# Two batches' query groups in one 512-column product for seven of twelve portions of a gate-and-value layer

## The chip, the cores and the metric

The kernel runs on one core of a Trainium2 chip. The metric is the time of one execution on the device, in microseconds (us); shorter is better.

## What is computed

Causal attention with a decaying bias, and then two gated expert layers on all tokens; the first normalises its input.

```python
x = attention(q, k, v, s)               # 4 batches, 8 heads, 576 tokens, 64 wide
x = x.transpose(0, 2, 1, 3).reshape(4 * 576, 512)
xn = x / sqrt(mean(x * x) + 1e-6) * rms_g
x = (silu(xn @ w_gate) * (xn @ w_val)) @ w_out      # 512 -> 1536 -> 512
return (silu(x @ w2_gate) * (x @ w2_val)) @ w2_out  # 512 -> 1536 -> 512
```

All is float32. A product is made of three: each factor is split into a high part H and a rest L, and HH + HL + LH is summed.

## The kernel before

**Groups.** The 576 queries of a batch are two groups, A (256 queries) and B (320). The change concerns group A of batches 0 and 1, called 0A and 1A here; 0B is group B of batch 0, and so on. Attention comes in the order 0A, 1A (`attend_early`), 0B, 1B, and then batches 2 and 3 with both groups at once. After a group's attention `normalise` turns its columns into `xH` and `xL` (512 features in four blocks k of 128 rows), in one of two slots: slot 0 holds 0A and then 0B, slot 1 holds 1A and then 1B, and so on.

**The first expert layer.** `moe1` makes the hidden features in twelve portions f of 128. A portion of a group is called a row here ("0A5" is portion 5 of 0A). `gate_value` makes its gate and its value: each 4 blocks k times 3 matmuls (HH, HL, LH), so 24 matmuls (L1071), into two of four rotating PSUM banks `mo`. `hidden` then takes one ScalarE operation (L1078) and two of VectorE (L1080, L1083), and the result goes to memory.

**What sets the order.** A planner (`Plan.run`) lists all operations by their dependences, a cost for each, and a priority, and writes one fixed order for each engine. Attention stands before rows: rows of 0A and 1A have the priority `P_MOE + f`, behind all attention, so they fill TensorE (PE) where attention leaves it free. `hidden` has the highest priority. A row can only be placed once its group is normalised and its weights are loaded.

**Steps that the prediction names**, all in `normalise`: L1038 and L1039 (VectorE) write the factors of the rows, L1043 transposes them (PE), L1046 (ScalarE) copies them into the last block of the slot's own `xL`, L1051 spreads them over the features (PE), L1055 (VectorE) multiplies, L1058 (ScalarE) writes `xH`, L1060 (POOL or VectorE) writes `xL`. As L1046 writes into the slot, it must wait until the last row of the group that held the slot before has read it. In attention, L651 and L776 are scores, L720 and L795 transposes, L732 values. L1440 is a product of the layer's second half, with 512 columns.

Of the kernel before, what the change touches and what calls it, by code (L numbers as in the profile page):

```python
# [11 lines left out]
F32R = mybir.dt.float32r  # L12
# [5 lines left out]
ACTF = mybir.ActivationFunctionType  # L18
ALU = mybir.AluOpType
# [4 lines left out]
P = 128  # L24
DM, DFF = 512, 1536
KD, KF = DM // P, DFF // P
# [8 lines left out]
GROUPS = {"A": (0, 256, (0, 1)), "B": (256, 320, (2, 3, 4))}  # L35
# [5 lines left out]
PE, DVE, ACT, POOL, SP, NONE = "PE", "DVE", "ACT", "POOL", "SP", "NONE"  # L41
# [38 lines left out]
class Plan:  # L80
# [20 lines left out]
    def op(self, eng, ns, fn, r=(), w=(), pri=0.0, later=0, port=False, slow=0.0):  # L101

        n = len(self.ops)
        done = 0
        if eng == SP:  # L110
            took = ns / self.RATE
            ns = max(450.0, took)
            done = 2300.0 + took - ns + slow
        deps, shared = set(), []
        for accesses, writes in ((r, False), (w, True)):
            for a in accesses:
                buf, part = a if isinstance(a, tuple) else (a, None)
                key = buf if isinstance(buf, str) else buf.key
                live = self.live.setdefault(key, [])
                keep = []  # L120
                for part2, m, wrote in live:
                    meets = part is None or part2 is None or part == part2
                    if meets and (writes or wrote) and m != n:
                        deps.add(m)
                    if not (writes and meets and (part is None or part == part2)):
                        keep.append((part2, m, wrote))
                keep.append((part, n, writes))
                self.live[key] = keep
                if not isinstance(buf, str) and buf.share is not None and buf not in shared:
                    shared.append(buf)  # L130
                    buf.uses += 1
        engs = eng if isinstance(eng, list) else [(eng, ns)]
        self.ops.append((engs, fn, deps, pri, done, shared, later, port))
        return n
# [132 lines left out]
def c_mm(n):  # L267
    return max(72.0, 0.4167 * n + 13.3)
# [6 lines left out]
def c_tt(n):  # L275
    return 75 + 1.04 * n
# [6 lines left out]
def c_act(n, aps=0):  # L283
    return 60 + 0.83 * n + 93 * aps
# [16 lines left out]
def tile_kernel(  # L301
# [16 lines left out]
    op = plan.op  # L318
# [32 lines left out]
    def bank(tag):  # L351
        return buf("ps", tag, [P, 512], F32)
# [49 lines left out]
    P_CONV, P_MOE, P_ATT = -1.0e3, 1.0e4, 0.0  # L402
# [55 lines left out]
    def raw_places(last):  # L458

        return {(f, z): buf("w", f"{'HL'[z]}{f + 2}", [P, 1024], I32, f"raw{z}")  # L460
                if f + 2 < KF else last[z] for f in range(KF) for z in range(2)}

    def load_gv(src, f, places, tmps, pri, early=None, after=()):
        H, L = (buf("w", f"{z}{f}", [P, 1024], F32R) for z in "HL")
        for z in range(2):
            convert(src[f, :, 512 * z:512 * z + 512], (H, L), z, places[f, z], tmps(), pri,
                    early, after)
        return H, L
# [451 lines left out]

    xHL = [[buf("m1", f"x{z}{i}", [P, KD, 320], F32R) for z in "HL"] for i in range(2)]

    def normalise(i, g, tot, pri, split=True):
        pri -= 2
# [134 lines left out]
                out=L()[:, k, :n], in0=x()[:, k, :n], in1=f32(H()[:, k, :n]), op=ALU.subtract),  # L1061
               r=halves + [(H, k)], w=[(L, k)], pri=pri, port=True)

    def gate_value(ps, W, X, f, z, n, pri, also=(), after=()):

        wH, wL = W
        xH, xL = X
        for k in range(KD):
            c = slice((z * KD + k) * P, (z * KD + k + 1) * P)
            for i, (a, x) in enumerate(((wH, xH), (wH, xL), (wL, xH))):  # L1070
                op(PE, c_mm(n), lambda en, a=a, x=x, c=c, k=k, i=i: en.matmul(  # L1071
                    ps()[:, :n], a()[:, c], x()[:, k, :n], start=(k == 0 and i == 0),
                    stop=(k == KD - 1 and i == 2)), r=[(a, z), (x, k), *after],
                   w=[ps] if k or i else [ps, *also], pri=pri)

    def hidden(gp, vp_, t, hh, n, pri):

        op(ACT, c_act(n), lambda en: en.activation(t()[:, :n], gp()[:, :n], ACTF.Tanh, scale=0.5),  # L1078
           r=[gp], w=[t], pri=pri)
        op(DVE, c_tt(n), lambda en: en.scalar_tensor_tensor(  # L1080
            out=t()[:, :n], in0=t()[:, :n], scalar=1.0, in1=gp()[:, :n], op0=ALU.add,
            op1=ALU.mult), r=[gp, t], w=[t], pri=pri)
        op(DVE, c_tt(n), lambda en: en.tensor_tensor(  # L1083
            out=hh()[:, :n], in0=t()[:, :n], in1=vp_()[:, :n], op=ALU.mult),
           r=[vp_, t], w=[hh], pri=pri)

    h_parts = {}

    def moe1(groups, W, pri, post, deep=None, hook=None):

        for f in range(KF):
            for b, g, i in groups:
                q0, n, _ = GROUPS[g]
                tok = b * S + q0
                k = next(deep) if deep else 0
                if k % 2:
                    gp, vq = (bank(f"{('sps', 'tp')[k // 2 % 2]}{z}") for z in range(2))
                    t, hh = deep_t[k // 2 % 2]
                else:
                    gp, vq = mo_bank(), mo_bank()  # L1100
                    t = shared("m1", "t", 2, [P, 320], F32)
                    hh = shared("m1", "hh", 2, [P, 320], F32)
                gate_value(gp, W[f], xHL[i], f, 0, n, pri + f, [vq, f"row {b}{g}{f}"])
                gate_value(vq, W[f], xHL[i], f, 1, n, pri + f)
                hidden(gp, vq, t, hh, n, post)
                for t0, m, gi, at in SPANS:
                    lo, hi = max(t0, tok), min(t0 + m, tok + n)
                    if lo < hi:
                        h_parts.setdefault(gi, set()).add(lo)
                        op(SP, 4 * P * (hi - lo),  # L1110
                           lambda en, gi=gi, lo=lo, hi=hi, t0=t0 - at, tok=tok, f=f, hh=hh: en.dma_start(
                               out=h_d[gi][f, :, lo - t0:hi - t0], in_=hh()[:, lo - tok:hi - tok]),
                           r=[hh], w=[(f"h_d{gi}", (f, lo))], pri=post, later=1200)
            if hook is not None:
                hook(f)

# [1 line left out]
    W1 = []  # L1120
    plan.live["ex"] = []
    places = raw_places([buf("ex", f"ex{i}", [P, 1024], I32, f"cvs{i}") for i in range(2)])
# [10 lines left out]
    def attend_early(b, x, tot):  # L1133
        for h in range(NH):
            units.append(None)
            pri = P_ATT + len(units) - 1
            u = EarlyUnit(b, h, x, tot)
            u.load(pri - 1000)
            u.scores(pri)
            u.values(pri - 0.6)  # L1140
            if u.i == 3:
                later()
        normalise(x, "A", tot, P_ATT + len(units), False)
# [35 lines left out]

    attend_early(0, 0, totals[0])  # L1180
    attend_early(1, 1, totals[1])
    AHEAD = 12

    def load_next(f, after=()):

        if f < KF:
            W1.append(load_gv(w_gv, f, places, tmps1, P_ATT + 8 + 1.5 * f,
                              P_ATT - 1000 + 8 + 1.5 * f, after))
    for f in range(AHEAD):
        load_next(f)  # L1190
    moe1([(0, "A", 0), (1, "A", 1)], W1, P_MOE, -1.0e4,
         hook=lambda f: load_next(f + AHEAD, [f"row 0A{f}"]))
    attend(0, "B", [0])
    attend(1, "B", [1])
    moe1([(0, "B", 0)], W1, P_MOE + 100, -1.0e4)
# [192 lines left out]
    deep = itertools.count()  # L1388
    b = wide("ex2", [P, 1024], F32, "t")
# [353 lines left out]
    for p in range(NPAIR):  # L1743
# [5 lines left out]
        b, c, d = (two_banks("sps0", "sps1"), two_banks("tp0", "tp1"), two_mo()) if p == 0 else \  # L1749
# [32 lines left out]
    for tag in w2_tags[0]:  # L1782
        b = wide(tag, [P, 2048], F32R, "wo")
# [30 lines left out]
    t = [two(tag, F32, "oo") for tag in U_TAGS]  # L1814
# [64 lines left out]
```

## Time and profile before

| | |
|---|---|
| median of 3 runs | 1060.56 us (1059.48 to 1063.21) |
| the profiled execution, its own time | 1061.81 us |
| its span, first to last instruction | 1060.0 us |
| PE busy | 1039.3 us (98%), 6308 instructions |
| VectorE, ScalarE, POOL busy | 74%, 61%, 25% |

PE's matmuls overlap in their pipelines: one of 256 columns is shown for 0.28 us, and the next begins 0.12 us after it. A busy share therefore hides short gaps, and the cost of a matmul is read from the distance between starts, or from a merged piece of many.

### The profile page before, as it was taken

The numbers are of one execution on the slowest core, as the hardware profiler recorded it, in microseconds if no ns is written. First come the engines' busy times: TensorE is split into PE (matmuls) and PEld (weight loads), VectorE is DVE, ScalarE is ACT, GpSimd is POOL, SyncE is SP. The second block draws the span as 40 slices with busy tenths as digits, with TensorE's granted clock in tenths as the row PEclk, the third lists the DMA queues.
The fourth block names the chain that finished last, engine by engine and source line by source line (L and its number), as shares of the span: only waits on it lengthen the run. The fifth ranks groups of instructions, "written<-read, shape, count | busy, mean of one in ns | idle before, by whom it ended". The sixth has DMA issues, their size and how long they took to land.

```text
span 1060.0 us, 19434 instructions
## 1 busy us (share of the span) xinstructions
PE 1039.3 (98%) x6308; PEld 937.0 (88%) x6308; DVE 782.2 (74%) x1881; ACT 642.8 (61%) x1375; POOL 262.4 (25%) x360
## 2 busy tenths in 40 slices
PE   7999999999999999999999999999999999999998
PEld 5789999999999999999987889888888888878888
DVE  7899778777788776766778888566567766876562
ACT  6978778767763665433366766554566544664652
POOL 4367655533442530000000000212113120200000
PEclk9999999999999999999999999999999999999999
DMA  7886455543656831656587672676757668878673
GB/s 218 262 278 191 134 150 148 153 117 106 184 152 199 246 94 50 218 186 229 191 290 253 196 228 62 226 228 196 251 190 253 233 222 279 277 256 268 212 233 112
DMA packets 127383, 211.17 MB, mean 199 GB/s; under 512 B 16112, under 2 KB 55024, under 8 KB 127280
## 3 DMA queue, kind: packets, MB, share of 16 engines
q1 hardware_dynamic: 126656, 209.58, 62.6%
q8 instruction: 50, 0.82, 0.3%
q14 instruction: 53, 0.43, 0.1%
q10 hardware_dynamic: 624, 0.34, 0.1%
HBM read 145.29 MB, written 64.56 MB: 198 GB/s over the span
## 4 chain that ended last, share of the span: by engine, by line
PE 58%; DVE 3%; DMA 3%; ACT 1%; issue 1%; SPq 0%; ACTq 0%; DVEq 0%
PE mo L1610 10%; PE mo L1071 9%; PE sps L1610 9%; PE mo L1440 8%; PE tp L1440 5%; PE sps L1440 5%; PE mo L1686 3%; PE sps L1071 2%; PE tp L1071 2%; PE mo L1495 2%; PE tp L1610 1%; PE sps L1495 1%; PE tp L1495 1%; DVE hL L1336 1%; DMA hh<-h_d 1%; PE tp L732 1%
## 5 line engine op out<-in xcount | busy, mean ns | idle before, releaser
L1071 PE MATMUL mo<-xL,H 128*128 128x256 f32 (+1 forms) x672 | 201.5, 300 | 0.9 <-DVE xL L1060 0.9
L1071 PE MATMUL mo<-xH,H 128*128 128x256 f32 (+1 forms) x672 | 201.2, 301 | 0.3 <-DVE hh L1083 0.2
L1071 PE MATMUL mo<-xH,L 128*128 128x256 f32 (+1 forms) x672 | 200.7, 300 | 0.0
L1336 DVE TENSOR_TENSOR hL<-hh,hH 128x512 fp32r<-128x512 f32 (+1 forms) x192 | 126.3, 669 | 69.8 <-ACT hH L1333 69.0
L1333 ACT ACTIVATE hH<-hh 128x512 fp32r<-128x512 f32 (+1 forms) x192 | 115.2, 603 | 93.5 <-DVE hL L1336 22.6
L1071 PEld LDWEIGHTS mo<-xL,H 128*128 128x128 f32 x672 | 127.5, 190 | 1.9 <-DVE xL L1060 1.1
L1071 PEld LDWEIGHTS mo<-xH,H 128*128 128x128 f32 x672 | 127.3, 190 | 1.2 <-ACT xH L1058 0.7
L1071 PEld LDWEIGHTS mo<-xH,L 128*128 128x128 f32 x672 | 127.3, 190 | 0.1
L688 ACT ACTIVATE sc<-sc,col 128x128 f32<-128x128 f32 (+3 forms) x128 | 73.0, 571 | 55.5 <-DVE col L677 54.6
L1440 PE MATMUL mo<-hH,wo 128*128 128x512 f32 x312 | 97.9, 390 | 0.0
L1440 PEld LDWEIGHTS mo<-hH,wo 128*128 128x128 f32 x312 | 58.6, 188 | 12.4 <-ACT hH L1333 0.3
L1078 ACT ACTIVATE t<-mo 128x256 f32<-128x256 f32 (+1 forms) x84 | 34.0, 405 | 47.7 <-PE mo L1071 42.8
L1440 PE MATMUL mo<-hL,wo 128*128 128x512 f32 x156 | 61.0, 391 | 0.6 <-DVE hL L1336 0.6
L1616 ACT ACTIVATE u<-sps 128x512 f32<-128x512 f32 x48 | 28.5, 594 | 54.2 <-PE sps L1610 54.2
L1440 PE MATMUL tp<-hH,wo 128*128 128x512 f32 x192 | 60.4, 389 | 0.0
L732 PE MATMUL tp<-pTB,vst 128*128 128x320 f32 (+2 forms) x320 | 52.5, 295 | 2.2 <-DVE pTB L725 1.4
L1440 PE MATMUL sps<-hH,wo 128*128 128x512 f32 x168 | 53.2, 390 | 0.4 <-ACT hH L1333 0.4
L725 DVE TENSOR_TENSOR pTB<-tp,pTB 128x512 fp32r<-128x512 f32 x64 | 43.5, 687 | 12.5 <-ACT pTB L723 12.0
L1080 DVE SCALAR_TENSOR_TENSOR t<-t,mo 128x256 f32<-128x256 f32 (+1 forms) x84 | 37.7, 449 | 19.7 <-ACT t L1078 18.9
L732 PEld LDWEIGHTS tp<-pTB,vst 128*128 128x128 f32 x320 | 46.6, 189 | 4.6 <-DVE pTB L725 3.2
L720 PE MATMUL tp<-ident,sc 128*128 128x128 f32 x304 | 46.9, 274 | 1.5 <-DVE x L741 1.1
L1625 ACT ACTIVATE u<-u 128x512 f32<-128x512 f32 x48 | 29.6, 631 | 29.6 <-DVE u L1620 29.5
(283 smaller groups left out, 2892.6 us busy)
## 6 DMA issues: line engine op xcount, KB each, us to landing
raw<-in_w_gv SPq DMA_DIRECT2D x44, 511.8 KB, 5.4
tb<-h_d SPq DMA_DIRECT2D x48, 256.0 KB, 3.9
t<-tb SPq DMA_DIRECT2D x48, 256.0 KB, 2.6
hh<-t SPq DMA_DIRECT2D x48, 256.0 KB, 3.3
lq<-in_qk SPq DMA_DIRECT2D x32, 288.0 KB, 3.8
cb<-cum_d SPq DMA_DIRECT2D x32, 288.0 KB, 3.7
hh<-h_d SPq DMA_DIRECT2D x36, 256.0 KB, 3.4
h_d<-hh SPq DMA_DIRECT2D x54, 128.0 KB, 2.2
```

Of the source, the lines that this page charges most:

```text
L688: op(ACT, c_act(o + m, 2) + 35, lambda en: en.activation(sc()[:m, :o + m], sc()[:m, :o + m], ACTF.Exp, scale=-1.0, bias=col()[:m, 0, t:t + 1],
L720: op(PE, C_TR, lambda en, pt=pt, a=a, kb=kb, t=t: en.transpose(pt()[:, a * P:a * P + P], self.sc[t]()[:, kb * P:kb * P + P], ident()), r=[ ...
L725: op(DVE, c_tt(n), lambda en, pt=pt, c=c: en.tensor_tensor(out=place(L, c), in0=source(pt, c), in1=f32(place(H, c)), op=ALU.subtract), r=[ ...
L732: op(PE, c_mm(n), lambda en, w=w, z=z, kb=kb, d0=d0, n=n, o=o: en.matmul(po()[:, o:o + n], vst[j]()[:, kb, :], pT[g][z]()[:, d0:d0 + n], s ...
L1071: op(PE, c_mm(n), lambda en, a=a, x=x, c=c, k=k, i=i: en.matmul(ps()[:, :n], a()[:, c], x()[:, k, :n], start=(k == 0 and i == 0), stop=(k ...
L1078: op(ACT, c_act(n), lambda en: en.activation(t()[:, :n], gp()[:, :n], ACTF.Tanh, scale=0.5), r=[gp], w=[t], pri=pri)
L1080: op(DVE, c_tt(n), lambda en: en.scalar_tensor_tensor(out=t()[:, :n], in0=t()[:, :n], scalar=1.0, in1=gp()[:, :n], op0=ALU.add, op1=ALU.mu ...
L1333: op(ACT, c_act(n) + 35, lambda en: en.activation(H(), src(), ACTF.Copy), r=[src, *after], w=[H], pri=pri)
L1336: lambda en: en.tensor_tensor(out=L(), in0=src(), in1=f32(H()), op=ALU.subtract),
L1440: op(PE, c_mm(n), lambda en, m=m, w=w, xx=xx, kk=kk, i=i: en.matmul(ps[m]()[:, :n], w(), xx(), start=first and kk == 0 and i == 0, stop=kk ...
L1495: op(PE, c_mm(n), lambda en, dd=dd, w=w, xx=xx, f=f, i=i: en.matmul(acc[dd]()[:, :n], w(), xx(), start=f == 0 and i == 0, stop=f == KF - 1 ...
L1610: op(PE, c_mm(n), lambda en, w=w, xx=xx, cut=cut, kk=kk, i=i: en.matmul(ps()[:, :n], W[w]()[:, cut], xx(), start=first and kk == 0 and i == 0,
```

## The change

For portions 0 to 4 the rows of 0A and 1A stay as they are, and they are written down batch by batch. For portions 5 to 11 one matmul now takes the columns of both slots, 2 x 256 = 512, into one PSUM bank. For that, the slots become halves of one tile. `hidden` still runs for each batch by itself, on its half of the bank. The loop that loaded weights some portions ahead is written more simply, and loads the same in the same order of priority (its lead was 12 of 12).

```diff
-    xHL = [[buf("m1", f"x{z}{i}", [P, KD, 320], F32R) for z in "HL"] for i in range(2)]
+    xB = {z: buf("m1", f"x{z}", [P, 2, KD, 320], F32R) for z in "HL"}
...
-    def gate_value(ps, W, X, f, z, n, pri, also=(), after=()):
+    def gate_value(ps, W, slots, f, z, n, pri, also=(), after=()):
...
+        N = n * len(slots)
+
+        def moving(y, k):
+            if len(slots) == 1:
+                return xHL[slots[0]]["HL".index(y)]()[:, k, :n]
+            return xB[y]()[:, :, k, :n]
...
-                op(PE, c_mm(n), lambda en, a=a, x=x, c=c, k=k, i=i: en.matmul(
-                    ps()[:, :n], a()[:, c], x()[:, k, :n], start=(k == 0 and i == 0),
+                op(PE, c_mm(N), lambda en, a=a, y=y, c=c, k=k, i=i: en.matmul(
+                    ps()[:, :N], a()[:, c], moving(y, k), start=(k == 0 and i == 0),
...
-    moe1([(0, "A", 0), (1, "A", 1)], W1, P_MOE, -1.0e4,
-         hook=lambda f: load_next(f + AHEAD, [f"row 0A{f}"]))
+    for f in range(KF):
+        W1.append(load_gv(w_gv, f, places, tmps1, P_ATT + 8 + 1.5 * f, P_ATT - 1000 + 8 + 1.5 * f))
+    APART = 5
+    for i in range(2):
+        moe1([(i, "A", i)], W1, P_MOE, -1.0e4, rows=range(APART))
+    moe1([(0, "A", 0), (1, "A", 1)], W1, P_MOE, -1.0e4, rows=range(APART, KF))
```

The planner makes a new order of this. Two places of PE's queue are shown; the lines of the new program lie lower (L1071 is L1081 there, L1051 is L1056).

The first is the end of row 0A4 (`mo1_1003`; `H4`, `H5` are weights of portions 4 and 5, `xH0` is slot 0). Before:

```order
L1071 MATMUL mo1_1003<-xH0_672,L4_620 128x256
L1071 MATMUL mo3_1039<-xH0_672,H5_721 128x256
L1071 MATMUL mo3_1039<-xL0_642,H5_721 128x256
L651 MATMUL sps1_1044<-kHH0_712,qst0_751 128x384
L651 MATMUL sps0_1048<-kHH1_785,qst1_799 128x288
L651 MATMUL sps0_1048<-kLL1_837,qst1_799 128x288
L651 MATMUL sps1_1044<-kLL0_756,qst0_751 128x384
L1071 MATMUL mo3_1039<-xH0_672,L5_733 128x256
L1071 MATMUL mo3_1039<-xH0_672,H5_721 128x256
L1071 MATMUL mo3_1039<-xL0_642,H5_721 128x256
L1071 MATMUL mo3_1039<-xH0_672,L5_733 128x256
L1071 MATMUL mo3_1039<-xH0_672,H5_721 128x256
```

And now:

```order
L1081 MATMUL mo1_1003<-xH_672,L4_620 128x256
L651 MATMUL sps1_1039<-kHH0_712,qst0_751 128x384
L651 MATMUL sps1_1039<-kLL0_756,qst0_751 128x384
L651 MATMUL sps0_1044<-kHH1_785,qst1_799 128x288
L651 MATMUL sps0_1044<-kLL1_837,qst1_799 128x288
L732 MATMUL tp1_1049<-pTB0_1006,vst0_778 128x320
L732 MATMUL tp1_1049<-pTB1_1019,vst0_778 128x320
L732 MATMUL tp1_1049<-pTB0_1006,vst0_778 128x320
L732 MATMUL tp1_1049<-pTB1_1019,vst0_778 128x320
L720 MATMUL tp0_1064<-ident_144,sc20_858 128x128
L720 MATMUL tp0_1064<-ident_144,sc40_273 128x128 x3
```

Rows 0A5, 0A6 and 0A7 stood among the attention of 0B that follows here. Now nothing of the layer stands in the next 56 matmuls and transposes of PE, up to row 1A0, since portion 5 waits for 1A as well.

The second is the end of portion 11 and the way to 0B's first row. Before, at the end of 1A11 (`xH1` is slot 1; 0A11, the last row of 0A, had ended before 1A11 began):

```order
L651 MATMUL sps1_2810<-kHH0_712,qst0_751 128x288
L651 MATMUL sps1_2810<-kLL0_756,qst0_751 128x288
L1071 MATMUL mo2_2756<-xL1_1245,H11_1608 128x256
L776 MATMUL sps0_2816<-kHH0_712,qst0_751 128x448
L776 MATMUL sps0_2816<-kLL0_756,qst0_751 128x448
L776 MATMUL sps0_2816<-kHH1_785,qst1_799 128x448
L776 MATMUL sps0_2816<-kLL1_837,qst1_799 128x448
L1071 MATMUL mo2_2756<-xH1_1297,L11_1621 128x256
L1051 MATMUL mo1_2829<-xL0_642,sel_253 128x320
L720 MATMUL tp1_2831<-ident_144,sc21_2618 128x128
L720 MATMUL tp1_2831<-ident_144,sc41_275 128x128 x3
L732 MATMUL tp0_2840<-pTB0_1006,vst1_820 128x320
```

And now, at the end of the joined portion 11:

```order
L1081 MATMUL mo0_2574<-xH_672,H11_1656 128x512
L1081 MATMUL mo0_2574<-xL_642,H11_1656 128x512
L1081 MATMUL mo0_2574<-xH_672,L11_1664 128x512
L720 MATMUL tp1_2634<-ident_144,sc21_2420 128x128
L720 MATMUL tp1_2634<-ident_144,sc41_275 128x128 x3
L732 MATMUL tp0_2643<-pTB0_1006,vst1_820 128x320
L732 MATMUL tp0_2643<-pTB1_1019,vst1_820 128x320
L732 MATMUL tp0_2643<-pTB0_1006,vst1_820 128x320
L732 MATMUL tp0_2643<-pTB1_1019,vst1_820 128x320
L651 MATMUL sps0_2655<-kHH1_785,qst1_799 128x288
L651 MATMUL sps0_2655<-kLL1_837,qst1_799 128x288
L651 MATMUL sps1_2659<-kHH1_785,qst1_799 128x384
```

Before, the 24 matmuls of 1A11 stood between the end of 0A11, which frees slot 0, and 0B's first row. Now the joined portion frees slot 0 only at its end, and 26 matmuls of attention and `normalise` are all that follows up to 0B's first row. Further down, row 0B6, which stood before the rows of 1B, now stands behind them; from the first row of batch 2 on PE's order is nearly the same as before, and from row 3B3 on the very same.

## Rows read from the trace of the kernel before

**Rows 1.** Part 2 of the page: PE's granted clock, 40 slices.

```profile
PEclk9999999999999999999999999999999999999999
```

**Rows 2.** Engines by stretch: busy us (count) of PE, PEld, DVE, ACT, POOL; clock; DMA.

```profile
67.00:87.00 20.00, 18.18 (x135) 16.80 (x134) 18.27 (x63) 18.27 (x44) 16.19 (x18) 1.00 0.79 238
87.00:302.00 215.00, 213.18 (x1599) 209.34 (x1599) 170.34 (x595) 160.24 (x403) 109.36 (x174) 1.00 0.49 145
302.00:325.00 23.00, 22.46 (x158) 21.69 (x158) 17.27 (x61) 11.22 (x30) 8.01 (x13) 1.00 0.69 203
325.00:330.00 5.00, 4.13 (x17) 2.43 (x15) 4.55 (x10) 2.66 (x7) 1.73 (x3) 0.95 0.55 173
```

**Rows 3.** The chain that ended last: start, us, merged pieces of PE.

```profile
490.70 3.52 PE tp L1071 x24
...
523.01 2.88 PE tp L1071 x24
...
592.81 8.16 PE tp L1440 x36
```

**Rows 4.** Stretches again, L1071 alone: PE and PEld busy, clock, DMA.

```profile
67.00:87.00 20.00, 11.34 (x75) 9.79 (x74) 1.00 0.79 238
...
302.00:325.00 23.00, 17.79 (x108) 16.02 (x108) 1.00 0.69 203
```

**Rows 5.** Timeline, PE, DVE and ACT, about normalising batch 1: start, us, what.

```profile
67.15 0.28 PE L1071 MATMUL mo<-xL,H 128*128 128x256 f32 x1
...
73.84 0.26 DVE L1038 CAST sq<-fac 128x16 fp32r<-128x16 f32 x1
...
77.50 0.39 ACT L1078 ACTIVATE t<-mo 128x256 f32<-128x256 f32 x1
...
77.92 0.42 DVE L1080 SCALAR_TENSOR_TENSOR t<-t,mo 128x256 f32<-128x256 f32 x1
...
78.26 0.17 DVE L1039 TENSOR_TENSOR sq<-fac,sq 128x16 f32<-128x16 f32 x1
...
81.14 0.41 DVE L1083 TENSOR_TENSOR hh<-t,mo 128x256 f32<-128x256 f32 x1
...
81.25 0.38 ACT L1046 ACTIVATE xL<-mo 128x256 fp32r<-128x256 f32 x1
...
83.92 0.86 DVE L1055 SCALAR_TENSOR_TENSOR x<-x,gcol,mo 128x256 f32<-128x256 f32 x2
...
84.75 0.71 ACT L1058 ACTIVATE xH<-x 128x256 fp32r<-128x256 f32 x2
...
86.83 0.55 PE L1071 MATMUL mo<-xH,H 128*128 128x256 f32 x2
```

**Rows 6.** Timeline, PE, ACT and DVE, from batch 0's last A row on.

```profile
171.00 0.28 PE L1071 MATMUL mo<-xH,L 128*128 128x256 f32 x1
...
171.78 0.43 ACT L1046 ACTIVATE xL<-mo 128x320 fp32r<-128x320 f32 x1
...
174.69 0.54 DVE L1055 SCALAR_TENSOR_TENSOR x<-x,gcol,mo 128x320 f32<-128x320 f32 x1
...
175.27 0.47 ACT L1058 ACTIVATE xH<-x 128x320 fp32r<-128x320 f32 x1 [0.23 <-DVE x L1055]
...
180.29 0.30 PE L1071 MATMUL mo<-xH,H 128*128 128x320 f32 x1
```

**Rows 7.** Timeline, PE, where batch 2 takes over.

```profile
325.77 0.90 PE L1051 MATMUL mo<-xL,sel 128*128 128x320 f32 x3
...
327.28 2.12 PE L1051 MATMUL mo<-xL,sel 128*128 128x256 f32 x5 [0.61 <-DVE hh L1083]
...
329.47 0.49 PE L1071 MATMUL mo<-xH,H 128*128 128x256 f32 x1
...
332.40 0.41 PE L1071 MATMUL mo<-xL,H 128*128 128x256 f32 x1
...
332.61 0.42 PE L1071 MATMUL mo<-xH,L 128*128 128x256 f32 x1
```

More of the change, by code (lines that the diff above doesn't have):

```diff
@@ L919, in values, with row_of @@
                r=[po], w=[(x, (k, o))], pri=pri)
-    xHL = [[buf("m1", f"x{z}{i}", [P, KD, 320], F32R) for z in "HL"] for i in range(2)]
+    xB = {z: buf("m1", f"x{z}", [P, 2, KD, 320], F32R) for z in "HL"}
+    def row_of(z, i):
+        return Buf(f"m1.x{z}{i}", lambda: xB[z]()[:, i])
+    xHL = [[row_of(z, i) for z in "HL"] for i in range(2)]
     def normalise(i, g, tot, pri, split=True):
@@ L1062, in normalise @@
                r=halves + [(H, k)], w=[(L, k)], pri=pri, port=True)
-    def gate_value(ps, W, X, f, z, n, pri, also=(), after=()):
+    def gate_value(ps, W, slots, f, z, n, pri, also=(), after=()):
         wH, wL = W
-        xH, xL = X
+        N = n * len(slots)
[3 more added lines that the diff above has]
+            return xB[y]()[:, :, k, :n]
         for k in range(KD):
             c = slice((z * KD + k) * P, (z * KD + k + 1) * P)
-            for i, (a, x) in enumerate(((wH, xH), (wH, xL), (wL, xH))):
-                op(PE, c_mm(n), lambda en, a=a, x=x, c=c, k=k, i=i: en.matmul(
-                    ps()[:, :n], a()[:, c], x()[:, k, :n], start=(k == 0 and i == 0),
-                    stop=(k == KD - 1 and i == 2)), r=[(a, z), (x, k), *after],
+            for i, (a, y) in enumerate(((wH, "H"), (wH, "L"), (wL, "H"))):
+                op(PE, c_mm(N), lambda en, a=a, y=y, c=c, k=k, i=i: en.matmul(
+                    ps()[:, :N], a()[:, c], moving(y, k), start=(k == 0 and i == 0),
+                    stop=(k == KD - 1 and i == 2)),
+                   r=[(a, z), *((xHL[j]["HL".index(y)], k) for j in slots), *after],
@@ L1074, in gate_value, with hidden @@
                    w=[ps] if k or i else [ps, *also], pri=pri)
-    def hidden(gp, vp_, t, hh, n, pri):
-        op(ACT, c_act(n), lambda en: en.activation(t()[:, :n], gp()[:, :n], ACTF.Tanh, scale=0.5),
-           r=[gp], w=[t], pri=pri)
+    def hidden(gp, vp_, t, hh, n, pri, lo=0):
+        op(ACT, c_act(n), lambda en: en.activation(
+            t()[:, :n], gp()[:, lo:lo + n], ACTF.Tanh, scale=0.5), r=[gp], w=[t], pri=pri)
         op(DVE, c_tt(n), lambda en: en.scalar_tensor_tensor(
-            out=t()[:, :n], in0=t()[:, :n], scalar=1.0, in1=gp()[:, :n], op0=ALU.add,
+            out=t()[:, :n], in0=t()[:, :n], scalar=1.0, in1=gp()[:, lo:lo + n], op0=ALU.add,
@@ L1082, in hidden, with moe1 @@
             op1=ALU.mult), r=[gp, t], w=[t], pri=pri)
         op(DVE, c_tt(n), lambda en: en.tensor_tensor(
-            out=hh()[:, :n], in0=t()[:, :n], in1=vp_()[:, :n], op=ALU.mult),
+            out=hh()[:, :n], in0=t()[:, :n], in1=vp_()[:, lo:lo + n], op=ALU.mult),
            r=[vp_, t], w=[hh], pri=pri)
     h_parts = {}
[L1089 to L1093, printed above, removed]
+    def moe1(groups, W, pri, post, deep=None, rows=range(KF)):
+        g = groups[0][1]
+        q0, n, _ = GROUPS[g]
+        slots = [i for _, _, i in groups]
+        for f in rows:
+            k = next(deep) if deep else 0
+            if k % 2:
+                gp, vq = (bank(f"{('sps', 'tp')[k // 2 % 2]}{z}") for z in range(2))
+            else:
+                gp, vq = mo_bank(), mo_bank()
+            gate_value(gp, W[f], slots, f, 0, n, pri + f,
+                       [vq, *(f"row {b}{g}{f}" for b, _, _ in groups)])
+            gate_value(vq, W[f], slots, f, 1, n, pri + f)
+            for j, (b, _, _) in enumerate(groups):
@@ L1094, in moe1 @@
                 tok = b * S + q0
-                k = next(deep) if deep else 0
                 if k % 2:
-                    gp, vq = (bank(f"{('sps', 'tp')[k // 2 % 2]}{z}") for z in range(2))
                     t, hh = deep_t[k // 2 % 2]
                 else:
-                    gp, vq = mo_bank(), mo_bank()
                     t = shared("m1", "t", 2, [P, 320], F32)
                     hh = shared("m1", "hh", 2, [P, 320], F32)
-                gate_value(gp, W[f], xHL[i], f, 0, n, pri + f, [vq, f"row {b}{g}{f}"])
@@ L1104, in moe1 @@
-                gate_value(vq, W[f], xHL[i], f, 1, n, pri + f)
-                hidden(gp, vq, t, hh, n, post)
+                hidden(gp, vq, t, hh, n, post, j * n)
                 for t0, m, gi, at in SPANS:
@@ L1113, in moe1 @@
                            r=[hh], w=[(f"h_d{gi}", (f, lo))], pri=post, later=1200)
-            if hook is not None:
-                hook(f)
     later = setup()
@@ L1181, in tile_kernel @@
     attend_early(1, 1, totals[1])
[L1182 to L1190, printed above, removed]
-    moe1([(0, "A", 0), (1, "A", 1)], W1, P_MOE, -1.0e4,
-         hook=lambda f: load_next(f + AHEAD, [f"row 0A{f}"]))
+    for f in range(KF):
[4 more added lines that the diff above has]
+    moe1([(0, "A", 0), (1, "A", 1)], W1, P_MOE, -1.0e4, rows=range(APART, KF))
     attend(0, "B", [0])
```

## The prediction

> **What bounds the kernel now.** I read first the clock, then the engines by stretch, then the chain that ended last, and then the timelines of the three places where the order changes.
>
> PE's clock stands at its full level, 2.4 GHz, in all 40 slices of the page [rows 1]; the one short fall lies in the stretch from 325 to 330 us, whose mean is 0.95 [rows 2]. Over the attention of batches 0 and 1, from 87 to 302 us, PE is shown busy for 213.18 of 215 us, while VectorE has 170 and ScalarE 160 [rows 2]. There PE's work is the bound, and rows of the layer are what fills it: 24 matmuls between steps of attention. Two stretches differ. From 67 to 87 us VectorE and ScalarE are at 18.27 of 20 us each, and PE has 135 matmuls, of which 75 are rows of the layer [rows 2, 4]; attention of 0B and the normalising of 1A are held there by the two slower engines, and PE is kept busy by the rows 0A5 to 0A7. And from 325.77 to 329.47 us PE has 8 matmuls only, since rows have run out and batch 2 is not yet normalised [rows 7].
>
> So the ledger is PE's: the time up to the first row of batch 2 (329.47) is PE's work plus what it stands idle, and behind that place the order hardly changes.
>
> **The change, part by part.**
>
> *The joined matmuls.* Twenty-four matmuls of 256 columns take 2.88 us in the chain, 0.120 us each; 36 of 512 columns take 8.16 us, 0.227 us each [rows 3]. A portion of both batches costs 2 x 2.88 = 5.76 us apart and 24 x 0.2267 = 5.44 us joined, so 0.32 us less, and seven portions 2.2 us less. The number of columns is the same; what goes away is some 13 ns that each matmul costs beside its columns. The bounds are 0, if a moving operand in two pieces of 256 columns costs as much as two matmuls (no row shows such an operand), and 2.2; I take 2.2, as the pieces are contiguous and the pitch within them is that of the rows measured.
>
> The Trainium skill, page "TensorE: Matmul & The Clock Gate", section "Back-to-back issue gap", gives N/2.4 + 2.5 ns from start to start at the full clock. By it a joined pair would save 2.5 ns, and the 168 pairs 0.4 us, an estimate by that page. The rows show 0.120 and 0.227 us where it has 0.109 and 0.216, so the trace disagrees, and it decides.
>
> *What does not change.* ScalarE and VectorE still run `hidden` for each batch: 0.39, 0.42 and 0.41 us for 256 columns [rows 5], the same 24 sets. Stores and weight loads are as many. The simpler loading loop is worth nothing, because its lead was all twelve portions before.
>
> *Rows 0A5 to 0A7 leave the stretch from 67 to 87 us.* They are 72 of the 75 matmuls of the layer there [rows 4]: 72 x 0.12 = 8.6 us of PE's work that now comes after 1A is normalised. PE has 56 instructions of attention and `normalise` in their place and otherwise waits. What comes back is that 1A is normalised earlier. Before, its factors are begun at 73.84 (L1038), finished at 78.26 (L1039), copied at 81.25 (L1046), used at 83.92 (L1055), written at 84.75 (L1058), and row 1A0 begins at 86.83 [rows 5]. Between L1038 and L1055 lie 10.1 us on VectorE. Five operations of `hidden`, at about 0.34 us from start to start, drop out of them, 1.7 us; in the new order an operand split and a weight step of that stretch stand elsewhere too, each at least twice as wide as L1080's 256 columns and so some 0.7 us by its 0.34, 1.4 us together; and three operations of `hidden` leave ScalarE. That is 3.1 us on VectorE and a shorter way through ScalarE and PE at each hand-over; I take 4 us earlier, so that 1A0 begins near 83. The bounds: 0, if the chain waits for attention's own steps at each place as it did; and 5.5, because ScalarE's 18.27 us less its three operations (0.9 us of engine time) and the weight steps that can be put off leave about 14.5 us. PE's added idle time is then 8.6 - 4.0 = 4.6 us, between 3.1 and 8.6.
>
> *The way from portion 11 to 0B's first row.* L1046 of 0B waits until slot 0 has been read. Before, 0A11's last matmul began at 171.00, L1046 at 171.78, L1055 at 174.69, `xH` of the first block was begun at 175.27, and 0B0 came at 180.29, with 1A11's 24 matmuls (2.9 us) in between [rows 6]. Now slot 0 is free only when the joined portion ends, and there is no row left to fill with. The chain from the last matmul to a first usable block takes at least 175.27 + 0.47 - 171.12 = 4.6 us, and about 0.3 us to PE (the step from L1046's start to L1055's has PE in it twice and is in that sum): 4.9 us. Behind the joined portion stand 26 matmuls and transposes, some 3.1 us at 0.12 us each. That leaves 1.8 us idle, and if the chain takes all of the 9.2 us up to 180.29, 6.1. A part of it was idle before too. I take 1.5 us more, between 0.5 and 6.
>
> *What is won back.* The three postponed rows have to be done later. Where PE is packed they just push the end; where it stood idle they cost nothing. Of the 23 us from 302 to 325, 108 matmuls of 320 columns take 108 x 0.147 = 15.8 us (3.52 us for 24) and the other 50 about 0.12 us each, 6.0 us, which leaves 1.2 us [rows 2 to 4]; one row more, 0B6, now lies in there. The 3.7 us before 329.47 are a chain of `normalise`, and PE's last rows stand ahead of it as before; from them I count nothing, and all 3.7 at most. From 87 to 302 us PE is shown idle for 1.8 us. I take 1.7 us won back, between 0 and 4.9.
>
> *The sum.* -2.2 + 4.6 + 1.5 - 1.7 = +2.2 us. It stands against the profiled execution's own 1061.81 us (span 1060.0), giving 1064.0; that execution lies 1.25 us above the median of the runs, 1060.56, so for a median I say **1062.8 us**. All bounds together would reach from -3.5 (-2.2 + 3.1 + 0.5 - 4.9) to +14.6 (0 + 8.6 + 6), but they would have to fall together.
>
> A measurement of this kernel can tell about 0.3%, 3.2 us, from no change.
>
> **The rivals.**
>
> *Rows deferred cost nothing: faster.* If attention and not PE sets the pace up to 329 us, the rows of the layer only have to be done by then. Then 1A's normalising 4 us earlier shifts everything behind it, the three sets of `hidden` that move into the later stretch give back 3 x 0.34 on ScalarE and 2 us at most on VectorE, and the 1.5 us at 0B may fall away. For it speaks that rows run out at 325.77 anyway and PE then waits 3.7 us [rows 7]. Against it speaks PE's 213 of 215 us [rows 2]. The price is -4.0 + 1.0 = -3.0, down to -4 if nothing is given back: 1056.6 to 1057.6 us. It decides if PE's idle time after 87 us falls by more than 4.6 us. Chance 0.18.
>
> *PE starves longer than I take: slower.* From 67 us on PE has less than half of its time filled. If 1A0 begins where it did (near 87), the idle term is 8.6 instead of 4.6 us, and the time 1066.8. The same stretch may also cost clock. The trace has one fall: after 3.7 us with 8 matmuls, the granted clock goes to its lower level, 1.2 GHz, and matmuls of 256 columns come 0.21 us apart (332.40 to 332.61) instead of 0.12 [rows 7]; some 16 of them, up to 333 us, lose 1.5 us in all. In the new stretch 56 instructions lie over 16 us, about seven in each 2 us, which is more than in that fall, so one fall is possible and not likely. It decides from a row 1A0 later than 85 us on, or a wait of over 4 us on the way to 0B0. Times from 1064 to 1068. Chance 0.30.
>
> *The join saves nothing.* If 512 columns from two pieces take 0.24 us, the 2.2 us fall away: 1065.0 us. Rows can't exclude it, but nothing in them has such a cost. Chance 0.05.
>
> **How the numbers follow.** The forecast has 0.47, with its own range of 1060 to 1066 us; by the bound of 3.2 us it is no change in 0.35 of these and slower in 0.12. The rival that is faster has 0.18, of which 0.14 pass the bound and 0.04 do not. The starving one has 0.30, with 0.19 slower and 0.11 not. The join that saves nothing has 0.05, 0.03 slower. Faster 0.14, and 0.02 for ends that I have not priced, makes 0.16; slower 0.34; no change 0.50. The range for 8 in 10 reaches from within the faster rival, 1056.5, to the end of the starving one, 1068.
>
> **What the profile after would show.** Right: joined matmuls 0.227 us from start to start; PE's busy count from 67 us to the first row of 1A at about 56, with 1A0 near 83 us; PE idle for one to three us before 0B0; the first row of batch 2 some 2 us later than 329.47, and all behind it shifted by the same. Wrong: the first row of batch 2 earlier than 327 us, which would say that attention sets the pace and PE has room; or 1A0 as late as 87 us; or a second fall of the granted clock near 75 us. What would make the forecast wrong without these is an order of ScalarE and VectorE after 87 us in which the pairs of `hidden` of a joined portion, two at a time, stand in attention's way.

## The result, and the profile after

The changed kernel takes 1067.49 us (median of 6 runs, 1063.89 to 1068.92) against 1060.89 us (6 runs, 1059.26 to 1063.21) for the kernel before on the same chip: a ratio of 1.0064, interval [1.0049, 1.008]. It is slower by some 6.6 us; the forecast was 2.2 us slower. The profiled execution took 1067.72 us with a span of 1065.7.

The page's clock line of the changed kernel, where [rows 1] had a 9 in every slice:

```profile
PEclk9989999999999999999999999999999999999999
```

The engines by stretch, with the columns of [rows 2]:

```profile
67.00:87.00 20.00, 15.35 (x83) 13.02 (x83) 16.92 (x62) 17.16 (x43) 14.02 (x19) 0.83 0.74 241
87.00:302.00 215.00, 212.09 (x1437) 199.92 (x1436) 174.14 (x585) 159.68 (x402) 101.77 (x167) 1.00 0.46 133
302.00:325.00 23.00, 21.98 (x154) 21.02 (x153) 16.50 (x59) 11.83 (x30) 7.32 (x11) 1.00 0.57 167
325.00:330.00 5.00, 5.00 (x36) 5.00 (x36) 4.41 (x17) 0.44 (x1) 0.00 (x0) 1.00 0.92 280
```

From 67 to 87 us PE has 83 instructions where it had 135, and the clock's mean falls to 0.83: the granted clock goes to 1.2 GHz at 72.5 us and stays there for 6.8 us. PE had then been without a row of the layer since 66.78. In all, the changed kernel runs three sets of 56 matmuls of 512 columns in place of 336 of 256. They begin 0.227 us apart, as forecast (timeline, PE):

```profile
113.34 0.39 PE L1081 MATMUL mo<-xH,L 128*128 128x512 f32 x1
113.57 0.39 PE L1081 MATMUL mo<-xH,H 128*128 128x512 f32 x1
...
115.15 0.39 PE L1081 MATMUL mo<-xL,H 128*128 128x512 f32 x1
115.38 0.39 PE L1081 MATMUL mo<-xH,L 128*128 128x512 f32 x1
```

The normalising of batch 1, in the timeline of the changed kernel (L1043 and L1044 were L1038 and L1039, L1051 was L1046, L1060 was L1055; compare [rows 5]):

```profile
66.78 0.28 PE L1081 MATMUL mo<-xH,L 128*128 128x256 f32 x1
...
72.97 0.98 DVE L1043 CAST sq<-fac 128x16 fp32r<-128x16 f32 x1
...
79.31 0.17 DVE L1044 TENSOR_TENSOR sq<-fac,sq 128x16 f32<-128x16 f32 x1
...
80.91 0.37 ACT L1051 ACTIVATE xL<-mo 128x256 fp32r<-128x256 f32 x1
...
82.19 1.65 DVE L1060 SCALAR_TENSOR_TENSOR x<-x,gcol,mo 128x256 f32<-128x256 f32 x4
82.97 0.71 ACT L1063 ACTIVATE xH<-x 128x256 fp32r<-128x256 f32 x2
...
83.43 0.86 PE L1081 MATMUL mo<-xH,H 128*128 128x256 f32 x4 [0.50 <-ACT xH L1063]
```

Row 1A0 begins at 83.43 us, 3.4 us earlier than in [rows 5], with 56 matmuls and transposes of PE between 66.78 and there. What PE waits for from 65 to 100 us is mainly attention itself, the copies of `pTB` by VectorE (the view of PE's waits; us in total, times, longest):

```profile
PE tp L732 <- DVE pTB L725: 2.1, 3, 1.0
PE sps L651 <- DVE col L677: 1.0, 1, 1.0
PE sps L651 <- DVE fac L1030: 0.8, 1, 0.8
PE tp L732 <- ACT pTB L804: 0.6, 1, 0.6
PE mo L1081 <- ACT xH L1063: 0.5, 1, 0.5
```

The way from portion 11 to 0B's first row, to be held against [rows 6] (timeline):

```profile
182.20 0.39 PE L1081 MATMUL mo<-xH,L 128*128 128x512 f32 x1
182.61 0.42 ACT L1051 ACTIVATE xL<-mo 128x320 fp32r<-128x320 f32 x1
...
185.77 0.47 ACT L1063 ACTIVATE xH<-x 128x320 fp32r<-128x320 f32 x1 [0.53 <-DVE x L1060]
...
186.58 0.54 PE L1081 MATMUL mo<-xH,H 128*128 128x320 f32 x2
```

The chain from the last reader of slot 0 to 0B0 takes 4.4 us now, from 182.20 on; it took 9.3 [rows 6]. Yet 0B0 comes 6.3 us later than before, because what stands ahead is later. And the place where batch 2 takes over, as in [rows 7]:

```profile
333.07 0.31 PE L1081 MATMUL mo<-xH,L 128*128 128x320 f32 x1
333.32 2.76 PE L1056 MATMUL mo<-xL,sel 128*128 128x320 f32 x8
336.14 0.35 PE L1081 MATMUL mo<-xH,H 128*128 128x256 f32 x1
```

2A0 begins at 336.14 instead of 329.47, 6.7 us later. The last gate-and-value matmul begins at 528.83 instead of 525.61, 3.2 us later, and the end is 5.7 us later. So a part is given back between 336 and 529, and 2.4 us are lost behind the last gate-and-value matmul, where the order did not change.

**Where PE stands unfilled.** For each stretch I sum PE's matmuls and transposes at the distance between starts that rows show for their shape at the full clock (0.119 us for 256 columns, 0.147 for 320, 0.227 for 512, 0.174 for 384, 0.203 for 448, 0.09 for a transpose, and so on) and take the sum from the stretch's length. What is left is time in which PE is idle or at its lower clock. The runs named in the head are those below.

| us | before | after | after again (E8) | eight apart (E2) | wait alone (E3) | five and the last apart (E9) |
|---|---|---|---|---|---|---|
| 65 to 100 | 5.0 | 11.8 | 13.0 | 5.1 | 11.5 | 12.1 |
| 100 to 180 | 5.0 | 3.7 | 3.7 | 5.0 | 3.3 | 3.8 |
| 180 to 200 | 0.9 | 2.0 | 2.2 | 1.1 | 1.8 | 0.8 |
| 200 to 240 | 2.8 | 5.3 | 6.6 | 3.2 | 3.7 | 1.9 |
| 240 to 300 | 2.3 | 2.3 | 2.4 | 2.3 | 2.7 | 3.2 |
| 300 to 340 | 7.0 | 5.0 | 4.9 | 5.6 | 2.8 | 5.5 |
| 340 to 400 | 5.7 | 2.9 | 2.8 | 2.7 | 2.2 | 3.5 |

The rows of 65 to 100 and of 200 to 240 hold the loss; behind 300 us a good part comes back. In the column of 200 to 240, E8 has a fall of the granted clock to 1.2 GHz at 231.1 us for 3.4 us, some 1.7 us of its 6.6; the changed kernel's first profile has none there.

### The profile page after: what moved, and what is told of

Same layout as the page of the kernel before. It is cut to its first block, busy times and chain, and to the rows that moved or that the text cites. A ratio compares the mean times of both kernels' runs of the same rounds, so it can differ in the third digit from the quotient of the medians.

```text
span 1065.7 us, 19106 instructions
## 1 busy us (share of the span) xinstructions
PE 1043.5 (98%) x6140; PEld 929.7 (87%) x6140; DVE 791.0 (74%) x1889; ACT 642.1 (60%) x1375; POOL 252.1 (24%) x352
## 4 chain that ended last, share of the span: by engine, by line
PE 51%; DMA 6%; DVE 5%; issue 2%; ACT 2%; SPq 1%; POOL 1%; ACTq 0%; DVEq 0%; POOLq 0%
PE mo L1081 9%; PE mo L1619 7%; PE mo L1449 7%; PE sps L1619 6%; PE sps L1449 4%; PE tp L1449 4%; PE mo L1695 2%; PE sps L1081 2%; PE tp L1081 2%; DMA raw<-in_w_gv 2%; PE mo L1504 2%; DMA tb<-h_d 1%; PE tp L1619 1%; PE tp L732 1%; DVE u L1648 1%
## 5 line engine op out<-in xcount | busy, mean ns | idle before, releaser
L1081 PE MATMUL mo<-xL,H 128*128 128x320 f32 (+2 forms) x616 | 191.7, 312 | 1.4 <-DVE xL L1065 1.2
L1081 PE MATMUL mo<-xH,H 128*128 128x320 f32 (+2 forms) x616 | 191.2, 312 | 0.7 <-ACT xH L1063 0.5
L1081 PE MATMUL mo<-xH,L 128*128 128x320 f32 (+2 forms) x616 | 191.1, 311 | 0.0
L1081 PEld LDWEIGHTS mo<-xL,H 128*128 128x128 f32 x616 | 116.4, 189 | 4.3 <-DVE xL L1065 1.9
L1081 PEld LDWEIGHTS mo<-xH,H 128*128 128x128 f32 x616 | 116.1, 189 | 3.3 <-ACT xH L1063 1.3
L1081 PEld LDWEIGHTS mo<-xH,L 128*128 128x128 f32 x616 | 116.4, 189 | 1.4
L688 ACT ACTIVATE sc<-sc,col 128x576 f32<-128x576 f32 (+3 forms) x128 | 73.0, 571 | 45.0 <-DVE col L677 43.9
```

What stands on the lines that cost most here:

```text
L688: op(ACT, c_act(o + m, 2) + 35, lambda en: en.activation(sc()[:m, :o + m], sc()[:m, :o + m], ACTF.Exp, scale=-1.0, bias=col()[:m, 0, t:t + 1],
L1081: op(PE, c_mm(N), lambda en, a=a, y=y, c=c, k=k, i=i: en.matmul(ps()[:, :N], a()[:, c], moving(y, k), start=(k == 0 and i == 0), stop=(k = ...
```

## The experiments

Each edit makes the planner write a new order of all that stands behind it, so a run changes more than its one line. Ahead of row 1B0, for instance, stand seven rows of 0B in the kernel before, six in the changed kernel, eight in E2, three in E3, four in E4, six in E5, seven in E6, E7 and E9, and five in E10.

Two theories. A: the loss comes from the order: rows put off behind batch 1's normalising leave PE without work, and it is not won back. B: the joined portions themselves cost (the pairs of `hidden`, banks, matmuls of two pieces).

**E1, nothing joined.** All the new code, with all twelve portions apart; PE's order is that of before.

```diff
-    APART = 5
+    APART = 12
```

> All twelve portions apart: the new code (one tile of two halves, rows written down batch by batch, the shorter loading loop) with nothing joined; PE's order is word for word that of before. Theory A (the loss comes from PE standing idle, since rows 0A5 to 0A7 wait for 1A): 1061 us, no change from before within 0.3%. Theory B (the joined portions themselves cost, by pairs of hidden and longer matmuls in attention's way): 1061 too. A time above 1064 would say that the shared tile costs by itself.

1061.52 us, ratio 1.0005 [0.999, 1.002] to 1060.87. The slots as halves of one tile and the simpler loading loop cost nothing that these runs can tell.

**E2, eight portions apart.** `APART = 8`: only portions 8 to 11 are joined, so that 0A5 to 0A7 stay where they filled PE.

> Portions 0 to 7 apart, 8 to 11 joined, so that rows 0A5 to 0A7 can again stand ahead of 1A. Theory A: four joined portions save 4 x 0.32 = 1.3 us, the way to 0B's first row still costs up to 2 us: 1060 to 1062 us. Theory B: four sevenths of the loss of 6.6 us stay, 1064.7 us.

1059.49 us, ratio 0.9989 [0.9973, 1.0005]. The stretch from 67 to 83 us is filled as before (columns as above):

```profile
67.00:83.00 16.00, 14.50 (x108) 13.41 (x107) 14.96 (x50) 13.78 (x31) 11.78 (x15) 1.00 0.83 252
```

Four joined portions in one kernel, and no loss: B falls as a cost of every joined portion, since it had 1064.7. The gain of 1.4 us is what four times 0.32 us gives, but the interval holds 1.

**E3, the wait alone.** The kernel with nothing joined, but rows 0A5 to 0A11 also name 1A's slot as an operand to wait for.

```diff
+            late = [(y, k) for y in xHL[1] for k in range(KD)] if (
+                groups == [(0, "A", 0)] and f >= 5) else []
+            gate_value(gp, W[f], slots, f, 0, n, pri + f,
-                       [vq, *(f"row {b}{g}{f}" for b, _, _ in groups)])
-            gate_value(vq, W[f], slots, f, 1, n, pri + f)
+                       [vq, *(f"row {b}{g}{f}" for b, _, _ in groups)], late)
+            gate_value(vq, W[f], slots, f, 1, n, pri + f, after=late)
...
-    APART = 5
+    APART = 12
```

> Nothing joined, but rows 0A5 to 0A11 are placed behind the normalising of 1A, as the join forces on them. Theory A: PE idle 5 to 6 us more from 67 to 83 us, with the same fall of the granted clock there, and 2 us of it won back: 1064 to 1066 us. Theory B: 1061 us.

1064.12 us, ratio 1.0036 [1.0022, 1.005]. The wait alone makes the kernel slower by 3.3 to 3.8 us (medians, ratio), with the starved stretch of the changed kernel: 58 PE instructions and a clock of 0.79.

```profile
67.00:83.00 16.00, 11.92 (x58) 9.73 (x58) 13.74 (x53) 13.73 (x32) 10.54 (x15) 0.79 0.83 258
```

So rows that wait for 1A make the kernel slower, as A has it, though not by the whole loss. The way from the wait to the time is shown less well. In this profile what the stretch loses is made up further on: the last gate-and-value matmul begins at 525.73, 0.1 us later than before, and 2.2 of the 2.3 us by which the span is longer lie behind it, in an order that is the same. One profile of each can't tell whether that part belongs to the wait.

**E4, the join undone.** The changed kernel with each joined product made as two of 256 columns in the same bank.

```diff
+        for j, slot in enumerate(slots):
...
+                        ps()[:, j * n:j * n + n], a()[:, c],
+                        xHL[slot]["HL".index(y)]()[:, k, :n], start=(k == 0 and i == 0),
...
```

> The changed kernel with its banks, pairs of hidden and waits for 1A, but each joined product made of two products of 256 columns, one slot after the other, in the same bank. Theory A: PE has the 2.2 us of work back that the join saves: 1069.7 us against 1067.5. Theory B, if longer matmuls in attention's way are the cost: 1064 or less; if 512 columns from two pieces cost as much as two matmuls: 1067.5.

1068.71 us, ratio 1.0083 [1.0061, 1.0105]: 1.2 us above the changed kernel as first measured and 0.6 above its second measurement (E8). The sign is that of the 2.2 us that the join was to save; the intervals overlap, and the order behind differs too, so the size is not shown by this run. What it does show is that the matmuls of 512 columns aren't what costs.

**E5, six portions apart.** `APART = 6`.

> Portions 0 to 5 apart, 6 to 11 joined: the rows 0A6 and 0A7, 48 matmuls or 5.8 us of PE's work, wait for 1A, and six portions save 0.32 us each, 1.9 us. Theory A (what is put off past 1A costs): between the changed kernel (1067) and the one with eight apart (1059.5), by the dose two thirds of the way, 1064 us, if PE's idle time grows with the rows put off. Theory B (each joined portion costs): six sevenths of 6.6 us, 1066.5 us.

1063.32 us, ratio 1.0035 [1.0021, 1.0049] to 1060.54. With eight, six and five portions apart the times are 1059.5, 1063.3 and 1067.5 us, in the order of the rows that stay in the starved stretch (108, 73 and 57 PE instructions from 67 to 83 us).

**E6, the last portion apart as well.** Portions 0 to 7 and 11 apart, 8 to 10 joined.

```diff
-    APART = 5
+    APART = [*range(8), KF - 1]
...
-    moe1([(0, "A", 0), (1, "A", 1)], W1, P_MOE, -1.0e4, rows=range(APART, KF))
+    moe1([(0, "A", 0), (1, "A", 1)], W1, P_MOE, -1.0e4, rows=range(8, KF - 1))
```

> Portions 0 to 7 and 11 apart, 8 to 10 joined: nothing waits for 1A that did not before, and 1A11 fills the way to 0B's first row again. If that way still cost something with eight apart, this is faster than 1059.5 by up to 1.5 us although one portion less is joined (0.3 us): 1058.5 us; if it cost nothing, 1059.8 us.

1059.23 us, ratio 0.9991 [0.9978, 1.0003], the same as E2. Where the early rows are in place, a joined last portion costs nothing that this can tell. E2 and E6 have the lowest medians of the study, 1.3 us below before; neither can be told from it.

**E7, the gap filled.** The changed kernel with 48 matmuls without use (rows 0A5 and 0A6 once more into banks that nobody reads) put where the old rows had been; E10 has 24 of them, 0A5's.

```diff
+    for f in range(APART, 7):
+        gp, vq = mo_bank(), mo_bank()
+        gate_value(gp, W1[f], [0], f, 0, 256, P_MOE + f, [vq])
+        gate_value(vq, W1[f], [0], f, 1, 256, P_MOE + f)
```

> The changed kernel with 48 matmuls of no use (the gates and values of rows 0A5 and 0A6, computed once more and thrown away) that the planner places in the stretch where PE waits for 1A. They keep PE busy there, and all that the join puts off stays put off. If the fall of the granted clock in that stretch is a part of the loss: no fall, 1A0 earlier by 1 to 2 us, 1065 to 1066 us against 1067. If the loss is the work put off alone: 1067 to 1068 us.

1065.58 us, ratio 1.0052 [1.0034, 1.007]. The clock stays up in that stretch, and falls once later, at 232.5 us for 3.4 us:

```profile
67.00:83.00 16.00, 13.47 (x96) 12.07 (x94) 15.34 (x48) 13.88 (x31) 9.73 (x12) 1.00 0.83 261
```

**E8, the changed kernel again**, beside E5 to E7 on their chip.

> The changed kernel once more, on the same chip as the others, for its time beside theirs and a second profile of it: 1066 to 1068 us, 1A0 near 83 us, the first row of batch 2 near 336 us, with a fall of the granted clock between 70 and 80 us.

1068.1 us, ratio 1.0075 [1.006, 1.0091]. E7 lies 2.5 us below, but the intervals overlap. Read by itself E7 would make the clock a share of the loss; E9 and E10 speak against it.

**E9, five portions and the last apart.** As E6, with `range(5)`: 5 to 10 joined.

> Portions 0 to 4 and 11 of the gate and value stay apart, 5 to 10 are joined: six joined portions in place of seven, so some 0.3 us less is saved, and the rows of 0A that are put off behind 1A are the same ones but for the last portion. If the way from the last portion to 0B's first row costs what the prediction gave it (1.5 us), the time is near 1066.3 us, 1.2 below the changed kernel. If that way costs nothing, as between the two kernels with eight portions apart, it is near 1067.8 us. The stretch from 67 to 83 us should look as in the changed kernel either way.

1064.0 us, ratio 1.0039 [1.0021, 1.0057] to 1060.72: 3.5 us under the changed kernel, more than either case had; its interval lies below that of E8 and overlaps a little with that of the first measurement. The starved stretch is as bad, and its clock is lower than in any other run, at 1.2 GHz for 10.2 us:

```profile
67.00:83.00 16.00, 12.75 (x57) 10.91 (x56) 13.24 (x51) 13.04 (x30) 9.96 (x14) 0.68 0.84 254
```

In the profiles the gain comes later. From 180 to 200 us PE is unfilled for 0.8 us instead of 2.0, which is the way to 0B0, and from 200 to 240 us for 1.9 instead of 5.3. Here is the way to 1B's first row in the changed kernel (timeline; L1056 spreads, L1060 multiplies, L1063 and L1065 write `xH` and `xL`; L606 and L603 prepare keys and queries for attention that comes later):

```profile
225.77 0.46 PE L1056 MATMUL mo<-xL,sel 128*128 128x320 f32 x2
...
226.03 1.43 POOL L606 TENSOR_TENSOR kLL<-lq,kHH 128x576 fp32r<-128x576 f32 x1 [5.80 <-ACT kHH L599]
...
226.30 0.54 DVE L1060 SCALAR_TENSOR_TENSOR x<-x,gcol,mo 128x320 f32<-128x320 f32 x1
...
226.90 0.81 PE L1056 MATMUL mo<-xL,sel 128*128 128x320 f32 x2
...
227.53 1.55 POOL L603 TENSOR_TENSOR qst<-lq,qst 64x640 fp32r<-64x640 f32 x1
...
228.74 1.77 DVE L1065 TENSOR_TENSOR xL<-x,xH 128x320 fp32r<-128x320 f32 x2
...
230.57 0.42 PE L1081 MATMUL mo<-xL,H 128*128 128x320 f32 x1 [0.37 <-DVE xL L1065]
```

And in E9:

```profile
225.93 0.31 PE L1056 MATMUL mo<-xL,sel 128*128 128x320 f32 x1
...
228.63 0.31 PE L1056 MATMUL mo<-xL,sel 128*128 128x320 f32 x1
...
229.36 0.31 PE L1056 MATMUL mo<-xL,sel 128*128 128x320 f32 x1
...
229.87 0.39 PE L1056 MATMUL mo<-xL,sel 128*128 128x320 f32 x1
230.20 0.38 PE L1081 MATMUL mo<-xH,H 128*128 128x320 f32 x1
```

In E9, row 0B6 (224.9 to 229.2 us) lies among the spreading matmuls, the first block of `xL` is written at 227.36 while PE works, and 1B0 runs on without a stop. In the changed kernel only six rows of 0B come before 1B0 instead of seven, the last matmul of 0B5 begins at 226.21, and 1B0 begins and stops again for `xL`. From 225 to 237 us PE runs 62 instructions there, and 86 in E9 (changed kernel, then E9):

```profile
225.00:237.00 12.00, 10.81 (x62) 8.71 (x61) 9.24 (x29) 6.53 (x16) 5.54 (x9) 1.00 0.25 79
```

```profile
225.00:237.00 12.00, 11.97 (x86) 11.55 (x85) 8.97 (x28) 7.98 (x20) 7.79 (x13) 1.00 0.44 126
```

Where 0B6 stands does not explain this by itself. E5 has six rows of 0B ahead of 1B0 like the changed kernel, none of their matmuls among the spreading ones, and is unfilled for 3.2 us from 200 to 240. The kernel before has seven rows ahead, but only four of their matmuls among the spreading ones, and is unfilled for 2.8; E7 has seven with one matmul there, and is unfilled for 5.8, its fall of the clock included. Another difference stands in the timelines. In the changed kernel POOL is taken by L606 and L603 from 226.03 to 229.08, and the first `xL` is begun at 228.74, 3.0 us after the first spreading matmul. In E5 these steps come earlier, and `xL` is begun 1.8 us after it (timeline):

```profile
223.67 1.57 POOL L603 TENSOR_TENSOR qst<-lq,qst 64x640 fp32r<-64x640 f32 x1 [3.58 <-ACT qst L601]
...
224.56 0.46 PE L1056 MATMUL mo<-xL,sel 128*128 128x320 f32 x2
...
226.35 1.95 POOL L1065 TENSOR_TENSOR xL<-x,xH 128x320 fp32r<-128x320 f32 x2 [1.12 <-ACT xH L1063]
```

No run moves these steps alone, or 0B6 alone, so what causes the loss from 200 to 240 us is not shown.

**E10, half of the filling.**

> The changed kernel with 24 matmuls without use (those of row 0A5's gate and value over again, nobody reads them) behind 0A4, in the stretch where TensorE waits for batch 1's normalising; it computes the reference. If the lower granted clock of that stretch is a part of the loss, and 24 matmuls keep it up, the time is 1065 to 1066 us, as with the 48 of the earlier run. If the clock is no part of the loss, or 24 do not keep it up, it is 1067 to 1068 us. The granted clock from 67 to 83 us tells the two apart.

1067.37 us, ratio 1.0079 [1.0051, 1.0107]. The clock was kept up through the stretch, and 1A0 came at 79.72 us, 3.7 us earlier than in the changed kernel; the time did not fall.

```profile
67.00:83.00 16.00, 12.40 (x85) 10.71 (x84) 14.71 (x51) 14.79 (x34) 11.53 (x15) 1.00 0.81 251
```

It is unfilled for 4.5 us from 85 to 100 instead, with a fall of the clock at 97.9 us for 3.4, and it has another at 231.1 us. With the useless matmuls counted at 0.12 us, the time from 65 to 100 that does nothing useful is 10.6 + 2.9 = 13.5 us in E10, 6.0 + 5.8 = 11.8 in E7, and 11.8 and 13.0 in the changed kernel's two profiles: much the same, with and without the fall of the clock in the starved stretch.

The mean granted clock of each execution says more. Three of E10's six have 1.000, so no fall of 3.4 us anywhere, and took 1066.6 to 1066.8 us; of the 70 executions of the kernel before that were measured beside E1 to E10, 16 have 1.000, with a median of 1058.6 us. So a loss of 8 us stands without any fall of the clock. Executions with a fall are the longer ones within a kernel: 41 of the kernel before have 0.998, with a median of 1060.9, and E10's other three took 1067.9 to 1070.5. Whether the fall costs that time or only comes with a longer wait is not shown. In the starved stretch a share of up to some 2 us, as E7's difference had it, isn't excluded.

## Why the prediction was right, and where its sizes were off

It was right in sign and in the mechanism that it put first, PE left without rows while batch 1 is normalised; the time lies above the likeliest case's own range (up to 1066), at the upper end of the whole range, where the rival of a starving PE stood. By its own bound of 3.2 us it had given a slower kernel 0.34 and no change 0.50. That the time lies inside the range is in part luck: up to the last gate-and-value matmul the errors of its terms nearly cancel, and the rest of the difference lies where it had counted nothing.

- **Joined matmuls, -2.2 us.** The step of 0.227 us was seen. The gain end to end is too small for these runs: E2 and E6 agree with 0.32 us a portion, E4 has the sign, but the intervals of E2 and E6 hold no change. The rival that the join saves nothing has the step against it. The Trainium skill, page "TensorE: Matmul & The Clock Gate", section "Back-to-back issue gap", has 0.216 us by its formula for the gap of an isolated matmul; the joined rows, at 0.227 us, disagree with it as those of before did.
- **Code that was to change nothing.** Right: E1.
- **PE idle near 1A's normalising, +4.6 us (3.1 to 8.6).** 1A0 near 83 and some 56 matmuls ahead of it came as forecast. From these alone it is 8.6 - 3.4 = 5.2 us. Up to 100 us the account shows 6.8 more than before, and 8.0 in the second profile: the term was 2 to 3 us too small, within its bounds. E3 prices this wait by itself, with all that is won back of it later, at some 3.6 us.
- **The way from portion 11 to 0B's first row, +1.5 us.** The account has +1.1 and +1.3 from 180 to 200 us: right. But the step stopped at 0B's first row. **This is what the prediction lacked**: the next hand-over, where 1B is normalised, had no term, and PE is unfilled there for 2.5 us more (3.8 in E8, with its fall of the clock). The row 0B6, which moved behind the rows of 1B, was counted only as work that turns up again from 302 to 325 us. It is not shown that its place makes this loss: E5 has the same place of it and is unfilled for 0.4 more than before. With the last portion apart (E9) both losses go, and with them 3.5 us of the time, for which the account has 1.2 and 3.4, less 1.9 that E9 is unfilled for more from 240 to 400 us.
- **Won back, -1.7 us (0 to -4.9).** It was 1.3 from 100 to 180, 2.0 from 300 to 340 and 2.8 from 340 to 400 us, 6.1 in all, and beyond the bound. From 87 to 302 us the prediction had read 1.8 us of idle time from PE's busy share, which hides short gaps; by the account PE is unfilled for 12 us there in the kernel before. I had also counted nothing behind the place where batch 2 takes over, since the order there hardly changes. But the fall of the clock at 329.5 us, 3.4 us long [rows 7], which not every execution of the kernel before has, did not occur, and a wait that before has at 366 us shrank. In the kernel before, VectorE waits there for loads of the layer's second half, and PE for VectorE (timeline):

```profile
366.41 1.22 DVE L1355 TENSOR_TENSOR tb<-tb 128x512 f32<-128x512 f32 x1 [2.73 <-DMA tb<-h_d]
...
367.90 0.47 PE L776 MATMUL sps<-kHH,qst 128*128 128x448 f32 x1 [0.64 <-DVE col L677]
369.07 0.69 DVE L1355 TENSOR_TENSOR tb<-tb 128x512 f32<-128x512 f32 x1 [1.23 <-DMA tb<-h_d]
...
370.64 0.63 PE L720 MATMUL tp<-ident,sc 128*128 128x128 f32 x4 [1.07 <-DVE x L741]
...
375.24 0.81 PE L732 MATMUL tp<-pTB,vst 128*128 128x320 f32 x5 [0.91 <-DVE pTB L725]
```

  PE's waits from 360 to 380 us are 2.6 us before and 0.2 us after.
- **The sum.** With the measured sizes, -2.2 + 6.8 + 1.1 + 2.5 - 6.1 + 0.6 (400 to 530 us) = +2.7 us up to the last gate-and-value matmul, which begins 3.2 us later; in E8's profile it begins 5.1 us later. The rest of the difference between the profiles, 2.4 and 2.0 us, is in the second half. There the order is the same in all, and from that matmul to the end the twelve profiles at hand take 533.1 to 538.1 us; E9's, of one of the shorter kernels, has the longest, and E10's the shortest. So this part varies between executions. Whether the changed kernel has more of it on average is open.
- **The rivals.** That deferred rows cost nothing is refuted by E3's time. The starving PE came true in its time and in its second fall of the clock, near 75 us, which I had called not likely, but 1A0 did not come as late as it had, and E9 and E10 do not bear out the clock as the cause. The orders of `hidden` in pairs, named last as a danger, have E2 against them, with four joined portions and no loss.

## What to carry to other kernels

A row that fills an engine while another group is normalised is paid for where it stands: before joining two pieces of work into one, list for each the waits that it covers, on every hand-over behind it, and not only the first. Joining only the work for which both operands have long been ready (portions 8 to 11 here) avoids the loss; the small saving that it should keep is within the noise of these runs. When a planner makes a new order, follow what each engine has in hand at the next hand-over, the steps of later groups included, and don't take one row that changes places (0B6) for the cause before a run has shown it.

## What the runs showed of the hardware

The granted clock fell to 1.2 GHz with PE far from idle. In the changed kernel it fell some six microseconds after the rows had ended, for 6.8 us, in a stretch with 57 PE instructions in 16 us. The prediction had called this possible and not likely; of the twelve profiles six have it in that stretch: the changed kernel twice and E3 for 6.8 us, E4 and E5 for 3.4, E9 for 10.2. A granted clock of 0.68 in such a stretch (E9) and one of 1.00 (E10) left nearly the same account, 12.1 us from 65 to 100 us and 13.5 with the useless matmuls counted as unfilled.
